# A transformer layer with linear attention: V products ahead of K in the head, fewer and longer dummy products, paced weight loads, and a newly searched order

## The chip, the cores and the metric

The kernel runs on one core of a Trainium2 chip. The metric is the device time of one execution in microseconds (us); it is measured several times and the median is taken. The core's engines are TensorE (PE, matrix products; its weight loads are listed as PEld), VectorE (DVE), ScalarE (ACT), GpSimd (POOL) and SyncE (SP, which here only issues transfers). Each engine works off its own list of instructions in order; between engines, semaphores make one wait for another.

## The reference

One layer over x of 2048 positions by 448 features, in bf16, with 16 heads of 28:

```python
qkv = (layernorm(x) @ wqkv)              # split into q, k, v per head
pq = einsum("bhsd,hdf->bhsf", q, w_phi)  # and pk from k, with the same w_phi
phi_q = concat([softmax(pq), softmax(-pq)], -1)   # phi_k likewise
kv = einsum("bhsf,bhsd->bhfd", phi_k, v)
z = einsum("bhsf->bhf", phi_k)
num = einsum("bhqf,bhfd->bhqd", phi_q, kv)
den = einsum("bhqf,bhf->bhq", phi_q, z)[..., None] + 1e-6
h = x + (num / den) @ wo
n = layernorm(h)
out = h + (sigmoid(n @ w_gate) * (n @ w_up)) @ w_down   # 448 -> 1792 -> 448
```

## The kernel before

The 2048 positions are 16 tiles of 128; four tiles make a chunk of 512. The names of the steps end in the number of their tile, or of chunk and part. The stages, as PE sees them:

- **Head.** The weights of K are transposed on PE (wT0 to wT3, copied out by wTe0 to wTe3), w_phi is spread on PE into a block matrix (wsp, masked by wex on DVE), and the product of the two, the folded weight, is made by w2m0_0 to w2m0_3 and cast to bf16 by w2e0_0 to w2e0_3. So K and w_phi are one product. The same is done for Q (w2m1_*, w2e1_*), whose weights come transposed by four transfers (ld_q0 to ld_q3, tile WqT). Meanwhile x is loaded (x0, x1, x2 ...), its statistics are taken (bst, agg on DVE), the reciprocal deviation made (pow1 on POOL) and the negated mean (nm1), x is normalized (xn) and transposed: tiles 0 to 3 on PE (xT0 to xT3, copied out by xT0e to xT3e), the others by transfers (xT4 to xT15 on SP's queue).
- **Keys and values, tiles 0 to 15.** For tiles 0 to 3 a pair of tiles shares a step: ppa0 and ppb0 are K of tiles 0 and 1, vva0 and vvb0 are V of tiles 0 and 1, ppa2 to vvb2 those of tiles 2 and 3. From tile 4 on, pva and pvb make K and V of one tile together. The a step has 8 products of 64 rows, run in pairs, and the b step 6. ACT takes both exponentials of K (ek), DVE sums and inverts them (ss, rs), POOL or DVE multiplies (phi), a copy brings V to SBUF (v1), and PE adds phi times V into two banks that stay open over all tiles (kva, kvb). At the end these are masked into kvz (kvzA to kvzD). One buffer of memory banks is shared by steps: ppa2 reuses the banks that ek0 and ek1 read, pva4 those that ek2 and v1_2 read.
- **Queries.** pqa and pqb make a chunk's part, ACT its two exponentials (eq, p and m for the signs). num makes numerator and denominator of a tile (rsm, qq, b, c, rden, o on DVE or POOL), o is transposed (oT, by PE for tiles 0 and 1, by transfers from tile 2), woa and wob multiply by wo; h, its statistics and norm follow (sq, ve, pow2, nm, hn), and its transpose hT (PE for tiles 0 and 1, transfers from tile 2).
- **Gate and up, down.** ga and gb make gate and up of a block of 128 features, ACT the tanh (sig), DVE the product (hh); dn, dp and dm multiply by w_down, fin adds the residual and out stores it.

What each engine does is written out by hand in `ORDER`, one list of names for each engine (lines 223 to 288). A step may run on one of several engines; it runs where its name stands. The dependences are worked out from the tiles that each step reads and writes, and waits are set for them; `PACE` adds dependences that no data asks for, here so that a weight load isn't issued too early. Steps whose function returns nothing (wwo, wgu) only make PE wait for weight loads. Dummy products of zeros (warm0 to warm9, line 524) fill PE in the head; each is n products of a given width:

```python
for i, (n, size) in enumerate(((4, 512), (1, 512), (1, 128), (2, 128), (1, 128), (6, 128), (4, 128), (6, 128), (8, 128), (2, 128))):
    op("pe", "warm%d" % i, warm(n, size), r=["zero"], w=[B(3)])
```

All products of two operands of 64 rows are issued by one helper, `both`, so that their line in the profile is L309.

Of the kernel before, what the change touches and what calls it, by code (L numbers as in the profile page):

```python
# [18 lines left out]
class Graph:  # L19
# [90 lines left out]
    def emit(self, nc):  # L110
# [111 lines left out]

ORDER = {
# [6 lines left out]
    ),  # L230
    "act": (
# [9 lines left out]
    ),  # L241
# [22 lines left out]
    ),  # L264
    "dve": (
# [14 lines left out]
    ),  # L280
    "pool": (
# [5 lines left out]
    ),  # L287
}
PACE = {"ld_wg1": "kva14"}
PROGRAM = (  # L290
# [35 lines left out]
def build(nc, A_x, A_wqkv, A_w_phi, A_wo, B_w_gate, B_w_up, B_w_down, out):  # L326
# [10 lines left out]
    with ExitStack() as es:  # L337
        def sb(name, shape, d=dt.bfloat16):
            return es.enter_context(nc.sbuf_tensor(name, shape, d))
        f32 = dt.float32  # L340
        ident = sb("ident", [P, P])
        zero = sb("zero", [P, 512])
        neghalf = sb("neghalf", [P, 4], f32)
        mask2 = sb("mask2", [P, 2], f32)
        par = sb("par", [P, 2])
# [10 lines left out]
        nm2 = sb("nm2", [P, NT], f32)  # L356
        ssq2 = sb("ssq2", [P, NT], f32)
        ve2 = sb("ve2", [P, NT], f32)
# [12 lines left out]
        zsel = sb("zsel", [GP, 452])  # L371
        hmask = sb("hmask", [GP, 4], f32)
# [148 lines left out]
        def warm(n, size):  # L521
            def f(e):
                for _ in range(n):
                    p = e.matmul(bk(3)[:, 0:size], lhsT=zero[:, 0:P], rhs=zero[:, 0:size], start=True, stop=True)  # L524
                return p
            return f
        for i, (n, size) in enumerate(((4, 512), (1, 512), (1, 128), (2, 128), (1, 128), (6, 128), (4, 128), (6, 128), (8, 128), (2, 128))):
            op("pe", "warm%d" % i, warm(n, size), r=["zero"], w=[B(3)])

        def evac(name, dst, src, rkey, wkey):  # L530
# [465 lines left out]
        at = {o.name: o.i for o in g.ops}  # L996
        for a, b in PACE.items():
            g.ops[at[a]].deps[at[b]] = False
# [36 lines left out]
```

## Time and profile before

| | us |
|---|---|
| median of 3 runs (lowest, highest) | 202.59 (202.31, 202.63) |
| the profiled execution | 202.7 |
| span of its instructions | 200.8 |
| PE busy | 195.5 |
| DVE busy | 132.0 |
| ACT busy | 89.4 |
| POOL busy | 56.2 |

The profile is of one execution; its span runs from the first instruction to the last, and the time of the execution holds some 2 us beside it. Line numbers (L309) are those of the kernel. A row of the timeline gives start, length, engine, line, operation, output and inputs, shapes, how many instructions are merged, and in brackets how long the engine was idle before and what released it. Products are pipelined, so a row's length is longer than what it adds before the next can start.

### The profile page before, as it was taken

What the parts mean: (1) busy time and instruction counts of PE and PEld (TensorE: products, weight loads), DVE (VectorE), ACT (ScalarE), POOL (GpSimd) and SP (SyncE); (2) the same over time, 40 slices, a digit from 0 to 9 for tenths busy, and PEclk for the clock granted to TensorE, in tenths of its full rate; (3) what the DMA queues carried; (4) which work ended last, traced back from release to release, by engine and by line L of the source; (5) the groups of instructions that cost most, each with busy time, mean ns of one, the idle gap of its engine ahead of it and who ended that gap; (6) DMA issues with size and microseconds to landing.
All of it is one profiled execution on the core that took longest, in us unless ns stands there. A gap on an engine that the chain in (4) does not pass through costs nothing.

```text
span 200.8 us, 5854 instructions
## 1 busy us (share of the span) xinstructions
PE 195.5 (97%) x2516; PEld 114.4 (57%) x2516; DVE 132.0 (66%) x308; ACT 89.4 (45%) x174; POOL 56.2 (28%) x95
## 2 busy tenths in 40 slices
PE   7999999999999999999999999999999999999995
PEld 4835556565568778787444444555555555554443
DVE  5999999978888986576569877346332422272224
ACT  2668988898883451434232432324323212222220
POOL 5779948633343207510170110001400000000000
PEclk9999999999999999999999999999999999999999
DMA  6965346749984230360015220020312000004002
GB/s 157 316 140 129 54 83 76 221 144 302 309 206 66 52 57 15 66 82 3 0 29 124 56 42 10 20 58 26 65 38 52 0 3 2 0 3 137 0 3 91
DMA packets 32490, 16.26 MB, mean 81 GB/s; under 512 B 24720, under 2 KB 31568, under 8 KB 32464
## 3 DMA queue, kind: packets, MB, share of 16 engines
q1 hardware_dynamic: 32336, 15.86, 33.7%
q8 instruction: 20, 0.33, 0.7%
q14 instruction: 6, 0.05, 0.1%
q10 hardware_dynamic: 128, 0.03, 0.1%
HBM read 8.34 MB, written 1.84 MB: 51 GB/s over the span
## 4 chain that ended last, share of the span: by engine, by line
PE 92%; ACT 3%; DMA 2%; issue 1%; SPq 1%; DVE 0%
PE psum L309 84%; PE psum L954 5%; DMA wk_sb<-in_A_wqkv_dram 2%; ACT hhT L671 1%; ACT eq L721 1%; ACT hhT L672 1%; PE psum L524 1%; PE psum L538 1%; PE psum L612 1%; SPq L413 1%; PE psum L599 0%; ACT xnT L531 0%; ACT v L531 0%; DVE x_sb L961 0%
## 5 line engine op out<-in xcount | busy, mean ns | idle before, releaser
L309 PE MATMUL psum<-xnT,wu_sb 64*128 64x512 bf16 (+1 forms) x490 | 93.6, 333 | 0.0
L309 PE MATMUL psum<-xnT,wg_sb 64*128 64x512 bf16 (+1 forms) x490 | 93.5, 333 | 0.1
L925 ACT ACTIVATE sg_sb<-psum 128x512 bf16<-128x512 f32 x56 | 33.2, 596 | 90.1 <-PE psum L309 89.5
L926 DVE SCALAR_TENSOR_TENSOR hhT<-sg_sb,psum 128x512 bf16<-128x512 bf16 x56 | 37.7, 684 | 52.1 <-ACT sg_sb L925 51.7
L309 PEld LDWEIGHTS psum<-xnT,wg_sb 64*128 64x128 bf16 x490 | 44.6, 94 | 20.9 <-DVE hhT L926 2.5
L309 PEld LDWEIGHTS psum<-xnT,wu_sb 64*128 64x128 bf16 x490 | 44.7, 94 | 13.9
L309 PE MATMUL psum<-wd_sb,hhT 64*128 64x448 bf16 x336 | 37.3, 349 | 0.0
L309 PEld LDWEIGHTS psum<-wd_sb,hhT 64*128 64x128 bf16 x336 | 17.8, 94 | 14.2 <-DVE x_sb L836 0.5
L309 PE MATMUL psum<-Wk,xnT 64*128 64x448 bf16 x112 | 22.2, 350 | 0.5 <-ACT hhT L672 0.2
L309 PE MATMUL psum<-wv_sb,xnT 64*128 64x448 bf16 x112 | 22.3, 351 | 0.1
L810 POOL TENSOR_TENSOR o_pad<-c_sb,rden 128x448 bf16<-128x448 bf16 x11 | 10.2, 935 | 28.5 <-DVE rden L806 28.4
L675 DVE TENSOR_REDUCE ss<-hhT 128x32 f32<-128x896 bf16 x16 | 16.8, 1060 | 0.2 <-ACT hhT L672 0.2
L721 ACT ACTIVATE eq<-psum 120x1024 bf16<-120x1024 f32 x16 | 15.6, 1030 | 0.6 <-PE psum L309 0.4
L685 POOL TENSOR_TENSOR phi<-hhT,rs 128x896 bf16<-128x896 bf16 x8 | 13.6, 1710 | 5.6 <-DVE rs L681 3.4
L309 PE MATMUL psum<-xnT,Wq 64*120 64x512 bf16 x112 | 14.8, 383 | 0.3 <-ACT eq L721 0.2
L845 POOL TENSOR_SCALAR ve<-ssq 128x1 f32<-128x1 f32 x11 | 2.2, 201 | 41.8 <-ACT junk L842 41.5
L309 PE MATMUL psum<-wo_o,oT 64*128 64x448 bf16 x56 | 13.2, 350 | 0.0
L309 PE MATMUL psum<-wo_e,oT 64*128 64x448 bf16 x56 | 13.2, 349 | 0.0
L961 DVE SCALAR_TENSOR_TENSOR x_sb<-psum,x_sb 128x448 bf16<-128x448 f32 (+2 forms) x17 | 9.4, 592 | 2.9 <-PE psum L954 1.6
L954 PE MATMUL psum<-wd_sb,hhT 128*128 128x448 bf16 (+2 forms) x70 | 11.2, 316 | 0.0
L309 PEld LDWEIGHTS psum<-Wk,xnT 64*128 64x128 bf16 x112 | 7.8, 94 | 5.8 <-PE psum L309 1.0
L671 ACT ACTIVATE hhT<-psum 128x448 bf16<-128x448 f32 x16 | 8.8, 553 | 4.4 <-PE psum L309 4.2
(105 smaller groups left out, 234.4 us busy)
## 6 DMA issues: line engine op xcount, KB each, us to landing
out_dram<-x_sb SPq DMA_DIRECT2D x15, 112.0 KB, 1.8
x_sb<-in_A_x_dram SPq DMA_DIRECT2D x7, 224.0 KB, 4.2
wd_sb<-in_B_w_down_dram SPq DMA_DIRECT2D x7, 224.0 KB, 5.1
wg_sb<-in_B_w_gate_dram SPq DMA_DIRECT2D x3, 448.0 KB, 5.8
wu_sb<-in_B_w_up_dram SPq DMA_DIRECT2D x3, 448.0 KB, 5.7
wv_sb<-in_A_wqkv_dram SPq DMA_DIRECT2D x2, 224.0 KB, 4.7
wk_sb<-in_A_wqkv_dram SPq DMA_DIRECT2D x2, 196.0 KB, 4.1
wo_e<-in_A_wo_dram SPq DMA_DIRECT2D x1, 336.0 KB, 3.3
```

The lines of the kernel that those rows point to most:

```text
L309: p = e.matmul(o, lhsT=w, rhs=r, start=st, stop=sp, tile_position=(row, 0))
L413: return op(eng, name, lambda e: e.dma_start(dst, src), r=r, w=w, dma="in" if eng == "sp" else "ain", nring=48 if eng == "sp" else 8, kb=kb)
L671: e.activation(ek[:, s, :, 0, :], src, ACT.Exp)
L675: op("dve", "ss%d" % t, lambda e: e.tensor_reduce(ss[:, s, :].rearrange("p (b h) -> p b h", h=2), eks.rearrange("p b (d h) -> p b h d", h= ...
L685: return e.tensor_tensor(phi[:, sp, :, :, :].rearrange("p b a n -> p (b a) n")[:, :, 0:56].rearrange("p b (d h) -> p b d h", h=2), eks.rea ...
L721: op("act", "eq%d_%d%s" % (c, i, "pm"[sg]), lambda e, sg=sg: e.activation(eq[c][:, sg, 2 * i:2 * i + 2, :].rearrange("p g n -> p (g n)"), ...
L810: return e.tensor_tensor(o_pad[:, t % NO, off:off + D].rearrange("p (h d) -> p h d", h=H), c_sb[:, t % NS, :, 0:DH], rden[:, t % NS, :][:, ...
L845: op(("pool", "dve"), "ve%d" % t, lambda e: e.tensor_scalar(ve2[:, t:t + 1], ssq2[:, t:t + 1], 1.0 / D ** 3, EPS, op0=ALU.mult, op1=ALU.ad ...
L925: op("act", "sig" + nm, lambda e: e.activation(sg_sb[:, k, 0:W], bk(bg)[:, 0:W], ACT.Tanh, scale=0.5), r=[B(bg)], w=[("sg", k)])
L926: op("dve", "hh" + nm, lambda e: e.scalar_tensor_tensor(out=dst, in0=sg_sb[:, k, 0:W].rearrange("p (f n) -> p f n", n=N), scalar=1.0, in1= ...
L954: p = e.matmul(bk(b)[:, lo:hi], lhsT=hb[:, ff, TS(t)], rhs=wd_sb[:, ff, lo:hi], start=ff == 0, stop=ff == FT - 1)
L961: op("dve", "fin%d%s" % (t, nm), lambda e: e.scalar_tensor_tensor(out=h_sb[:, t, lo:hi], in0=bk(b)[:, lo:hi], scalar=0.5, in1=h_sb[:, t, l ...
```

## The change

The products and transfers of data are the same ones; what differs is their order, the engine of some steps, the dummies and the holds.

- On SP's queue the two loads of V's weights (ld_v0, ld_v2) pass the loads x4 and x6.
- On PE, vva0 and vvb0 come ahead of ppa0 and ppb0, and vva2 ahead of ppa2 and ppb2 (vvb2 behind them); the transposes xT2 and xT3 and the folds w2m1_0 to w2m1_3 stand between other steps than before, all four folds ahead of pva4.
- The dummies are 14 products instead of 35, in 8 steps instead of 10; from the sixth step on they are 384 or 512 columns wide instead of 128. warm2 and warm3 stand ahead of wsp.
- `PACE` holds ten weight loads back instead of one, each until a named product (three of the loads of w_down follow the last two holds in SP's queue).
- Steps change engine: w2e0_3, v1_13, oT1e, nm1_1, nm1_4 and kvzC go to ACT; wTe3, phi8, o1, o10, o11, kvzB, ve5, ve8, ve9, hn4, hn6 and nm5 to DVE; phi5, phi6, o7, nm3, hn3, nm1_8, ve4 and ve6 to POOL.
- The order of many steps is new up to about num14 of PE's list; from there on PE's list is the same.

Cut to the head of each list, the queue of SP, PE's list up to num3 and around wgu, the holds and the dummies:

```diff
     "sp": (
-        "x0 x1 ld_k0 ld_k2 x2 x4 x6 ld_v0 ld_v2 x8 x10 ld_q1 ld_q0 ld_q3 ld_q2 x12 xT4 x14 xT5 xT6 xT7 xT8 xT9 xT10 "
+        "x0 x1 ld_k0 ld_k2 x2 ld_v0 ld_v2 x4 x6 x8 x10 ld_q1 ld_q0 ld_q3 ld_q2 x12 xT4 x14 xT5 xT6 xT7 xT8 xT9 xT10 "
...
     "act": (
-        "wphi wTe0 wTe2 wTe3 w2e0_0 w2e0_1 w2e0_2 par ek0 xT3e ek1 v1_0 v1_1 nm1_6 ek2 ek3 v1_2 w2e1_1 v1_3 nm1_8 "
-        "w2e1_0 v1_4 ek4 w2e1_2 ek5 v1_5 w2e1_3 v1_6 ek6 nm1_12 v1_7 ek7 ek8 v1_8 eq0_0p ek9 v1_9 ek10 v1_10 ek11 "
...
+        "wphi nm1_1 wTe2 wTe0 w2e0_1 w2e0_3 w2e0_2 w2e0_0 v1_1 v1_0 nm1_4 xT3e par ek0 ek1 nm1_6 w2e1_0 w2e1_1 ek2 "
+        "v1_2 ek3 v1_3 w2e1_3 ek4 v1_4 ek5 v1_5 w2e1_2 v1_6 ek6 nm1_12 ek7 v1_7 ek8 v1_8 eq0_0p ek9 v1_9 ek10 v1_10 "
...
     "pe": (
-        "warm0 warm1 wsp warm2 xT0 wT0 wT1 wT2 warm3 wT3 xT1 w2m0_0 w2m0_1 warm4 warm5 w2m0_3 w2m0_2 warm6 warm7 "
-        "warm8 ppa0 ppb0 warm9 xT2 xT3 vva0 vvb0 ppa2 ppb2 vva2 seed vvb2 w2m1_0 w2m1_1 kva0 pva4 kvb0 pvb4 pva5 "
-        "w2m1_2 w2m1_3 pvb5 kva1 pva6 kvb1 kva2 pvb6 kvb2 pva7 pqa0_0 pvb7 pva8 kva3 pvb8 kvb3 pqb0_0 pva9 kva4 pvb9 "
...
-        "kvb14 kva15 kvb15 qs pqa1_1 num0 num1 pqb1_1 pqa2_0 num2 pqb2_0 pqa2_1 oT0 oT1 num3 pqb2_1 woa0 wob0 pqa3_0 "
-        "num4 pqb3_0 pqa3_1 pqb3_1 num5 hT1 hT0 woa2 ga0_2 ga0_0 ga0_1 num6 gb0_0 ga0_3 gb0_1 gb0_2 gb0_3 wob2 num7 "
...
-        "wob6 gb0_10 ga0_12 gb0_11 ga0_13 dn0_0 dn0_4 gb0_12 gb0_13 num9 ga2_2 ga2_3 dn0_8 gb2_2 gb2_3 ga2_0 ga2_1 "
...
+        "warm0 warm1 warm2 warm3 wsp xT0 wT1 warm4 wT2 wT3 wT0 warm5 xT1 w2m0_1 w2m0_3 warm6 warm7 w2m0_2 w2m0_0 vva0 "
+        "vvb0 ppa0 xT3 ppb0 xT2 vva2 w2m1_0 ppa2 w2m1_1 ppb2 vvb2 seed w2m1_3 w2m1_2 kva0 pva4 pvb4 pva5 kvb0 kva1 "
+        "pvb5 pva6 kvb1 kva2 pvb6 pva7 pqa0_0 pvb7 pva8 kvb2 kva3 pvb8 kvb3 pqb0_0 pva9 kva4 pvb9 pva10 kvb4 kva5 "
...
+        "pqa1_1 num0 pqb1_1 num1 pqa2_0 num2 pqb2_0 pqa2_1 oT1 oT0 pqb2_1 num3 woa0 wob0 pqa3_0 num4 pqb3_0 pqa3_1 "
+        "wgu pqb3_1 num5 hT1 hT0 woa2 ga0_2 ga0_0 ga0_1 num6 ga0_3 wwo gb0_0 gb0_1 gb0_2 gb0_3 wob2 num7 ga0_4 ga0_5 "
...
+        "wob6 ga0_12 ga0_13 num9 gb0_12 gb0_13 dn0_0 dn0_4 dn0_8 ga2_2 num10 ga2_3 dn0_11 ga2_0 ga2_1 dp0_0 gb2_0 "
...
     "dve": (
-        "zero hmask mask2 bst0 agg0 bst1 agg1 xn0 kvzones wex xT0e wTe1 bst2 bst3 xT1e agg3 w2e0_3 agg2 bst7 bst5 "
-        "bst4 xn2 agg5 agg4 agg7 bst6 xT2e agg6 ss0 bst8 rs0 bst9 bst10 bst11 ss1 agg8 agg9 rs1 agg11 agg10 ss2 phi1 "
...
-        "rsm7 rden6 qq7 h2 b7 h3 c7 rden7 o7 hh0_4 ve3 hh0_6 h4 nm2 h5 nm3 rsm8 hn2 hn3 qq8 hh0_8 h6 h7 b8 c8 rden8 "
...
+        "zero hmask mask2 bst0 agg0 bst1 agg1 xn0 wex wTe1 xT0e wTe3 bst2 bst3 xT1e agg2 agg3 bst5 bst4 bst6 agg5 "
+        "agg6 agg4 bst7 xn2 agg7 bst10 agg10 xT2e bst8 ss0 bst9 rs0 ss1 agg9 agg8 bst11 rs1 agg11 ss2 phi1 rs2 bst14 "
...
+        "h2 b7 h3 c7 nm2 rden7 hh0_4 hh0_6 h4 ve3 rsm8 h5 qq8 b8 c8 hn2 hh0_8 h7 h6 rsm9 qq9 rden8 hh0_10 nm4 b9 c9 "
...
     "pool": (
-        "ident0 steps phipad ident zsel neghalf pow1_0 opad0 pow1_1 nm1_1 xn1 epsl0 v1ones wqpad epsr0 pow1_3 nm1_3 "
-        "pow1_2 xn3 pow1_4 nm1_4 xn4 pow1_6 xn5 xn6 phi0 xn7 pow1_8 xn8 phi2 xn10 xn9 phi4 pow1_12 xn13 phi7 xn15 "
...
+        "ident0 steps phipad ident zsel neghalf opad0 wqpad epsr0 epsl0 pow1_0 v1ones pow1_1 xn1 nm1_3 pow1_3 xn3 "
+        "pow1_2 pow1_4 xn4 pow1_6 xn5 xn6 phi0 xn7 nm1_8 pow1_8 xn8 phi2 xn9 xn10 phi4 pow1_12 phi5 xn13 phi6 phi7 "
+        "xn15 phi9 phi10 phi13 o0 o2 o3 pow2_0 pow2_1 o4 o5 o6 nm3 o7 ve2 pow2_3 hn3 pow2_2 ve6 ve4 pow2_4 o9 ve7 "
...
-PACE = {"ld_wg1": "kva14"}
+PACE = {"ld_wg0": "pvb14", "ld_wu0": "pvb15", "ld_wg1": "kvb10", "ld_wu1": "kvb11", "ld_wg2": "kvb12", "ld_wu2": "kvb13", "ld_wg3": "kvb14",
+        "ld_wu3": "pqa1_1", "ld_wd0": "num1", "ld_wd2": "pqb1_1"}
...
-        for i, (n, size) in enumerate(((4, 512), (1, 512), (1, 128), (2, 128), (1, 128), (6, 128), (4, 128), (6, 128), (8, 128), (2, 128))):
+        for i, (n, size) in enumerate(((4, 512), (1, 512), (1, 128), (2, 128), (1, 128), (2, 384), (1, 512), (2, 384))):
```

71 rows, old and new, of the table ORDER are left out of this document.

## The prediction

> **What bounds the kernel now.** I read the page first, then stretches of the span, then the chain that ended last, then the timeline of the first 20 us engine by engine.
>
> ```profile
> span 200.8 us, 5854 instructions
> PE 195.5 (97%) x2516; PEld 114.4 (57%) x2516; DVE 132.0 (66%) x308; ACT 89.4 (45%) x174; POOL 56.2 (28%) x95
> 8.00:18.00 10.00, 9.46 (x114) 5.03 (x112) 9.80 (x27) 7.26 (x19) 8.32 (x12) 1.00 0.80 187
> 18.00:43.00 25.00, 24.98 (x426) 14.98 (x428) 24.63 (x48) 22.26 (x50) 17.72 (x15) 1.00 0.53 120
> 43.00:60.00 17.00, 16.28 (x303) 9.96 (x301) 13.98 (x39) 14.54 (x20) 5.74 (x7) 1.00 0.91 241
> 60.00:125.00 65.00, 64.90 (x950) 42.08 (x946) 48.98 (x130) 23.08 (x48) 16.25 (x29) 1.00 0.27 48
> 125.00:201.00 76.00, 73.41 (x676) 37.85 (x670) 29.15 (x54) 19.31 (x36) 3.04 (x8) 1.00 0.12 33
> ```
>
> The stretches give, after their length, busy time of PE, weight loads, DVE, ACT, POOL, then granted clock and DMA. PE is idle 0.02 us between 18 and 43 and 0.10 us between 60 and 125, at a granted clock of 1.00, so there the time is PE's list of products and no order of it helps. What can be gained lies before 18 us, where PE is kept busy partly by dummies (products of zeros, L524), and between 43 and 60 us, where PE is idle 0.72 us. DVE is as full as PE from 8 to 43 us (9.80 of 10 and 24.63 of 25): a lead won in the head survives only if DVE can be earlier too.
>
> ```profile
> 8.59 1.01 PE psum L524 x18
> 9.59 0.92 PE psum L309 x8
> ...
> 17.45 0.43 ACT v L531
> 17.89 0.14 issue
> 18.02 2.49 PE psum L309 x30
> ...
> 47.20 1.95 ACT eq L721 x2
> ...
> 49.19 1.07 PE psum L309 x8
> ...
> 58.21 65.46 PE psum L309 x960
> ```
>
> The chain (start, length, what) shows three places. At 8.59 it runs through a whole microsecond of dummies, until the keys of tiles 0 and 1 (ppa0) may start. At 18.02 pva4 starts, released by ACT's copy of V of tile 2 (v1_2). At 49.19 PE was waiting for the exponentials of the queries (eq, ACT).
>
> **The head, walked again.** The rows for it:
>
> ```profile
> 1.17 2.31 PE L524 MATMUL psum<-zero 128*128 128x512 bf16 x5 [1.17 <-DVE zero L417]
> 6.39 0.41 PE L599 MATMUL psum<-ident,wk_sb 112*112 112x112 bf16 x4 [0.16 <-DMA wk_sb<-in_A_wqkv_dram]
> 6.70 1.15 DVE L545 BATCH_NORM_STATS2 st<-x_sb 128x6 f32<-128x448 bf16 x2
> 7.19 0.61 PE L612 MATMUL psum<-Wphi,WkT 112*128 112x112 bf16 x8
> 7.69 1.72 ACT L531 CAST Wk<-psum 128x448 bf16<-128x448 f32 x3
> 7.77 0.41 DVE L531 COPY xnT<-psum 128x512 bf16<-128x512 bf16 x1
> 9.56 1.74 PE L309 MATMUL psum<-Wk,xnT 64*128 64x448 bf16 x14
> 11.34 0.54 ACT L671 ACTIVATE hhT<-psum 128x448 bf16<-128x448 f32 x1 [1.88 <-PE psum L309]
> 11.78 0.54 ACT L672 ACTIVATE hhT<-psum 128x448 bf16<-128x448 f32 x1
> 13.82 1.74 PE L309 MATMUL psum<-Wk,xnT 64*128 64x448 bf16 x14 [0.19 <-ACT hhT L672]
> 15.64 1.69 POOL L685 TENSOR_TENSOR phi<-hhT,rs 128x896 bf16<-128x896 bf16 x1
> 17.05 0.57 PE L612 MATMUL psum<-Wphi,WqT 112*128 112x112 bf16 x8
> 17.31 0.57 ACT L531 CAST v<-psum 128x448 bf16<-128x448 f32 x1
> ```
>
> *Dummies ahead of the spread of w_phi.* The first five dummies of 512 columns took 2.31 us with a drain of 0.2, some 0.42 each, so three of 128 moved ahead of it (warm2, warm3) cost 3 x 0.105 = 0.32 us at most. They end nothing: the transposes wT2 and wT3 wait at 6.39 for the second load of the keys' weights, and nothing that the spread delays is needed for them. If that load were 0.3 us earlier, this cover would be gone and 0.3 us the price. The 384-wide dummies, not in the trace, lie between 0.06 us (18 of 128 in 1.01) and 0.42 us; I take 0.16, three quarters of a 512 at the later, doubled rate.
>
> *Start of V.* From 6.39: three transposes of weights (0.2 each to issue), two 384-dummies (0.33), xT1 (0.22), four folds (the row at 7.19 has two, eight products, in 0.61 with the drain, so 0.2 each) and the three dummies warm6 and warm7 (0.53): 6.39 + 0.6 + 0.33 + 0.22 + 0.8 + 0.53 = 8.9. The other input of vva0 is xT1's copy: DVE now has wTe3 first (to 7.4), two statistics (1.15 less an overlap of 0.1), then that copy (0.41): 8.84. So V of tiles 0 and 1 starts at 8.9, where dummies stood, instead of K at 9.56.
>
> *Keys behind it.* A 14-product pair step issues in 1.6 us: 8.9 + 1.6 = 10.5 for ppa0. It needs all four casts of the folded weight, now all on ACT: three in a row took 1.72, so about 0.52 each: from the first fold's end at 7.97, done at 10.2, hidden under V by 0.3 us. K ends near 12.25 (the 1.74 of the row at 9.56), so the first exponential starts at 12.4 instead of 11.34, a loss of 1.06. Two tiles of exponentials (11.34 and 11.78 rows: 0.98 for one, overlapping a little) end at 14.25, and ppa2, which reuses their banks, starts at 14.3 instead of 13.82. PE is idle about 0.65 us before vva2 (xT2's copy) and 0.4 us before ppa2, which the before filled with work.
>
> *The gain of the order.* K of tile 2 ends at 16.0. ACT then does ek2, v1_2, ek3 instead of ek2, ek3, v1_2: 16.05 + 0.87 + 0.57 = 17.45 for v1_2, against 17.88. With the 0.14 us from copy to product that the chain shows, pva4 starts at 17.6 instead of 18.02: 0.42 earlier. By then all four folds of the queries' weights are done, where the before had done two; the other two stood behind pva5, 0.2 us each (17.05 row: two folds in 0.57 with the drain). The lead of PE's list at pva4 is 0.42 + 0.4 = 0.8 us. kva0 stands ahead of pva4 and needs phi0 (POOL, 1.69 long). Even started as late as before, at 15.64, it ends at 17.33, so it does not hold pva4.
>
> **What else moves in the head.**
>
> ```profile
> 4.05 0.94 SPq L413 DMA_DIRECT2D wv_sb<-in_A_wqkv_dram  x2
> 6.03 5.16 SPq L503 DMA_TRANSPOSE WqT<-in_A_wqkv_dram  x4
> wv_sb<-in_A_wqkv_dram SPq DMA_DIRECT2D x2, 224.0 KB, 4.7
> DMA to landing us min/median/max: 3.7/4.4/5.0
> ```
>
> On SP's queue V's two loads pass x4 and x6: issued 0.95 us earlier, the second near 3.6, and landing by 3.6 + 4.7 = 8.3, ahead of 8.9; without the move the second would land near 9.2 and V would wait 0.3 us. x4 and x6 take V's old place and with the same 4.7 land near 8.8 and 9.2; their statistics come at 9.0 and 10.0, behind xT1's copy and tile 3's mean: nothing, and 0.5 us if DVE were there earlier. The transposes of the queries' weights (last row: their time to landing) keep their place; the last issue is near 9.9, so they land by 13.6 to 14.9. The fold w2m1_0 now stands ahead of ppa2, at 13.7: between nothing and 0.8 us of wait; I take 0.1, since ppa2 itself may not start before 14.3.
>
> **From 18 to 60 us.**
>
> ```profile
> 36.53 0.62 DVE L531 CAST v<-psum 128x448 bf16<-128x448 f32 x1
> 42.22 1.14 DVE L685 TENSOR_TENSOR phi<-hhT,rs 128x896 bf16<-128x896 bf16 x2
> 45.86 0.63 PE L309 MATMUL psum<-kvz,eq 56*128 56x60 bf16 x32
> 50.63 0.58 ACT L531 COPY oT<-psum 128x512 bf16<-128x512 bf16 x1 [0.58 <-PE psum L538]
> 46.33 0.44 SPq L413 DMA_DIRECT2D wu_sb<-in_B_w_up_dram  x1
> wu_sb<-in_B_w_up_dram SPq DMA_DIRECT2D x3, 448.0 KB, 5.7
> 70.24 3.37 SPq L856 DMA_TRANSPOSE xnT<-hn_pad  x2
> 75.67 0.27 PE L309 MATMUL psum<-xnT,wg_sb 64*128 64x256 bf16 x1
> ```
>
> *DVE* starts its statistics of tiles 2 and 3 some 0.66 us later (7.36 for 6.70), but gives a cast of the folded weight (about 0.57, as ACT's) and one of V (0.53) to ACT, and phi5 and phi6 to POOL for phi8 (net 0.55). It ends phi15 about 1 us earlier, at 42.4, and PE wants it about 2 us ahead of num0 (45.86 before): at 42.9 with the lead. POOL pays 1.7 us for the added phi out of 7.3 idle (17.72 of 25); ACT pays a V copy of 0.55 out of 2.7 idle. So the 0.8 us carries through. kvb0 and kva1, and kvb2 and kva3, now stand together; no row prices that, between nothing and 0.2 us, and I take 0.1.
>
> *At 46 us* pqb1_1 passes num1 (two num steps issue in 0.45, so 0.22 each): the exponentials that the chain waits for start 0.2 us earlier. oT1's copy moves to ACT (0.58), whose idle time of 0.58 before that copy and 2.5 in the stretch (14.54 of 17) hides it; o1 goes from POOL to DVE. If ACT had no idle left there, the 0.58 would be the price.
>
> *The ten paced loads.* SP now waits for pvb14 to pqb1_1; behind it stand only the rest of the weights and the transposes of o, far later. The last gate or up load is issued after pqa1_1, which ends just ahead of num0: 44.9 now against 46.33, landing 5.7 later, near 50.6. PE asks for all of them (wgu) ahead of pqb3_1, some 1.7 us of steps before the row of 58.21, so near 55.4 with the lead. Cost nothing, 4.8 us of cover; gain nothing either.
>
> **The sum.** 0.8 + 0.1 + 0.2 = 1.1 us off a span of 200.8: 199.7. The profiled execution took 202.7, 1.9 more than its span, and the median is 202.59: I predict 201.5. From num14 on, PE's order is the same, so nothing is given back by the tail as written.
>
> **The rivals.**
>
> *The lead stops at DVE, ACT or the queries' transposes (chance 0.14).* DVE had 0.37 us of room in 25. If its list or ACT's exponentials run 0.5 to 1 us later than I walked, or w2m1_0 waits the 0.8 us, what remains is 0 to 0.4: 202.2 to 202.6, no change that can be measured (0.2%, 0.4 us, is about what a measurement of this kernel tells). For it: the first exponential is 1.06 us later. Against it: V's copies, formerly behind it, are already done.
>
> *Slower: hT3 late (0.10).* nm3 and hn3 move to POOL, behind o7, and hn2 behind c8, while ga2_2, which reads both transposes, keeps its place by the queue of PE and is reached 0.9 us earlier, near 74.8. The before issued hT2 and hT3 from 70.24 to 73.61 and used them at 75.67, so hT3 landed with 0 to 2.06 us to spare. It decides when hT3 lands after 74.8; each 0.1 us from there is 0.1 us of PE. If there was no margin and POOL's longer steps add 1 us, PE stands 75.67 + 1 - 74.8 = 1.9 us: 203.4. Against it: what hn2 and hn3 read is itself computed earlier with the lead.
>
> *Slower: the clock (0.06).* 0.42 us for 512 columns early, then 0.056 for 128, is a doubled rate. With 14 dummies for 35 and PE idle for 1.05 us in the 2 us around 13, the rate could halve: the 2.6 us of products up to 16.4 would take 2.6 more, 0.4 hidden behind ACT: 203.7. Against it: in the before the rate held between 6.4 and 7.2, which is nearly all transposes behind a wait, and through the wait of 0.19 at 13.82. [...]
>
> **How the numbers follow.** Forecast 0.70: 201.5, and between 200.8 (all of the 0.72 idle in 43 to 60 goes, and of that 0.2 is counted already, plus the 0.2 taken as 0.1 and nothing for w2m1_0) and 202.1 (the 0.5 us of the added dummies' and casts' bounds lost). No change 0.14, slower 0.16. The range from 200.8 to 202.8 takes in the rival of no change, with the 0.2 by which runs of before spread, and leaves out the slower ones and a little below.
>
> **What would show it.** Right: the first V product near 8.9, ppa0 near 10.5, the first exponential near 12.4, pva4 near 17.6, num0 near 44.9, the chain's wait for eq at 48.0, PE still full from 60 on. Wrong: pva4 not before 18.0; idle PE of over 0.2 us between 18 and 43; ga2_2 waiting for the transpose of hn; products of 512 columns at 0.42 us after 10 us.

## The result and the profile after

The changed kernel took 206.17 us (median; 205.21 to 206.59, 4 executions) against 202.45 us of the kernel before beside it. The ratio is 1.0178, interval 1.0162 to 1.0195: slower by 3.7 us, where 1.1 us of gain were forecast. Two executions at a mean granted clock of 0.992 took 206.6 and 206.5 us, two at 1.000 took 205.2 and 205.8. The profiled one is the first, with a span of 204.8. In what follows, an execution more than 1.5% above the fastest of its kernel is left out of the ratio, but not out of the median and the range: one of the kernel before with ten holds (206.32) and two of the same with 20 dummies fewer (206.79 and 205.86).

The page of the profile after, cut to its size, the granted clock in 40 slices of 5.1 us, and the packets of PE's own list of instructions (queue 8: how many, MB, share of the transfer engines):

```profile
span 204.8 us, 5810 instructions
...
PEclk9999999999699999999999999999999999999999
...
q8 instruction: 19, 0.31, 0.7%
```

The same stretches as before (length; busy PE, weight loads, DVE, ACT, POOL; granted clock, DMA):

```profile
8.00:18.00 10.00, 8.66 (x97) 4.11 (x94) 9.13 (x27) 7.72 (x21) 8.29 (x12) 1.00 1.08 195
18.00:43.00 25.00, 24.37 (x418) 14.04 (x416) 24.79 (x45) 22.09 (x49) 19.51 (x16) 1.00 0.51 118
43.00:60.00 17.00, 14.56 (x246) 8.86 (x246) 11.12 (x30) 12.03 (x18) 3.36 (x4) 0.90 0.65 186
60.00:125.00 65.00, 64.84 (x972) 41.34 (x970) 50.85 (x137) 25.53 (x50) 15.73 (x28) 1.00 0.30 62
125.00:201.00 76.00, 75.90 (x693) 38.77 (x690) 30.35 (x58) 20.51 (x38) 3.03 (x8) 1.00 0.10 27
```

PE is idle 0.63 us between 18 and 43 (before 0.02) and 2.44 us between 43 and 60 (before 0.72). The granted clock is 0.90 in that last stretch, and PE got through 246 products there instead of 303. From 60 us on it is full, as before. The chain that ended last (start, length, what) names three places:

```profile
10.01 4.21 DMA WqT<-in_A_wqkv_dram
...
29.19 1.38 DVE kvz L462
...
31.72 0.97 DVE xn_pad L574
...
35.63 0.05 issue
...
44.84 1.58 PE psum L310 x48
46.42 0.11 issue
46.54 2.90 PE psum L310 x65
49.44 1.92 issue
51.35 2.28 PE psum L310 x11
```

The queries' transposed weights hold the head (10.01). Two small DVE steps take some 1.9 us together more than usual (29.19, 31.72; their rows stand below). And at 49.44 PE stands for 1.92 us, with nothing in the profile that it waited for. That stop is in the middle of a step, as PE's timeline shows:

```profile
48.80 0.64 PE L310 MATMUL psum<-xnT,Wq 64*120 64x512 bf16 x3
51.35 2.28 PE L310 MATMUL psum<-xnT,Wq 64*120 64x512 bf16 x11 [1.92 <-issue]
53.56 1.03 PE L539 MATMUL psum<-ident,o_pad 128*128 128x128 bf16 x8
54.53 1.20 PE L310 MATMUL psum<-xnT,Wq 64*120 64x512 bf16 x6
55.80 0.35 PE L310 MATMUL psum<-x_sb,ident 64*128 64x448 bf16 x2
```

The rows hold pqb2_0 (6 products) and pqa2_1 (8). pqb2_0 has issued 3 of its 6 products and had every input that it needs, yet the other 3, and the 8 of pqa2_1 behind them, come 1.9 us later. Products and transposes are slow behind that: the granted clock is 0.50 from 51.84 to 55.25 us. woa0, the row at 55.80, stood at 51.66 before: 4.14 us late. num0 (46.54) had been 0.68 us late. From woa0 to the end of the span both kernels need 149.0 to 149.1 us.

### The profile page after: what moved, and what is told of

It reads as the page before. It is cut to its first block, busy times and chain, and to the rows that moved or that the text cites. A ratio compares the mean times of both kernels' runs of the same rounds, so it can differ in the third digit from the quotient of the medians.

```text
span 204.8 us, 5810 instructions
## 1 busy us (share of the span) xinstructions
PE 196.4 (96%) x2494; PEld 112.8 (55%) x2495; DVE 133.2 (65%) x309; ACT 91.1 (44%) x177; POOL 54.5 (27%) x91
## 4 chain that ended last, share of the span: by engine, by line
PE 81%; DVE 9%; SPq 4%; DMA 2%; issue 2%; ACT 0%
PE psum L310 75%; PE psum L955 5%; DVE ss L676 4%; SPq L414 2%; DMA WqT<-in_A_wqkv_dram 2%; SPq L504 2%; DVE phi L686 1%; DVE st L546 1%; DVE rs L682 1%; DVE xn_pad L574 1%; PE psum L539 1%; DVE kvz L462 1%; PE psum L613 0%; ACT hhT L672 0%; ACT hhT L673 0%
## 5 line engine op out<-in xcount | busy, mean ns | idle before, releaser
L811 POOL TENSOR_TENSOR o_pad<-c_sb,rden 128x448 bf16<-128x448 bf16 x9 | 8.4, 938 | 37.9 <-DVE rden L807 21.0
L310 PE MATMUL psum<-xnT,Wq 64*120 64x512 bf16 x112 | 16.2, 406 | 2.1 <-issue 1.9
L676 DVE TENSOR_REDUCE ss<-hhT 128x32 f32<-128x896 bf16 x16 | 16.6, 1049 | 0.3 <-ACT hhT L673 0.3
L686 POOL TENSOR_TENSOR phi<-hhT,rs 128x896 bf16<-128x896 bf16 x9 | 15.3, 1707 | 5.1 <-DVE rs L682 2.7
L802 DVE TENSOR_TENSOR b_sb<-psum,qq 128x464 bf16<-128x464 f32 x16 | 10.2, 636 | 0.7 <-PE psum L310 0.5
```

Of the source, the lines that this page charges most:

```text
L310: p = e.matmul(o, lhsT=w, rhs=r, start=st, stop=sp, tile_position=(row, 0))
L676: op("dve", "ss%d" % t, lambda e: e.tensor_reduce(ss[:, s, :].rearrange("p (b h) -> p b h", h=2), eks.rearrange("p b (d h) -> p b h d", h= ...
L686: return e.tensor_tensor(phi[:, sp, :, :, :].rearrange("p b a n -> p (b a) n")[:, :, 0:56].rearrange("p b (d h) -> p b d h", h=2), eks.rea ...
L802: op("dve", "b%d" % t, lambda e: e.tensor_tensor(h3(b_sb), OMv[:, :, :, 0:EV], h2(qq)[:, :, :, None].to_broadcast([P, NB, 8, EV]), ALU.mul ...
L811: return e.tensor_tensor(o_pad[:, t % NO, off:off + D].rearrange("p (h d) -> p h d", h=H), c_sb[:, t % NS, :, 0:DH], rden[:, t % NS, :][:, ...
```

## What stopped PE: the theory and its rivals

The stop falls where PE's list of instructions, by the packets of its queue, should have been refilled. That queue delivers 0.31 MB in 19 packets, 16 KB each, for 4,989 products and weight loads: one packet for about 260 of them. That queue 8 carries PE's list is read from this: its packets keep pace with PE, and all kernels of the study with 42 or 44 more of PE's instructions have 20 of them, the others 19. In the records of single packets, those around the stop come at 30.20, 37.65, 43.18, 50.76 us before and at 30.04, 40.26, 48.85, 52.62 after. Between 40.26 and 48.85 PE worked off some 400 instructions without a refill, and it stopped at the end of these. The transfers of that time in the changed kernel (41.4 to 48.8 us):

```profile
DMA packets 659, 2.05 MB, mean 278 GB/s; under 512 B 86, under 2 KB 86, under 8 KB 659
...
q1 hardware_dynamic: 659, 2.05, 100.7%
```

No packet of instructions is among them; the transfer engines are full with weights. Before, the same place (42.6 to 44.2 us) is empty but for the refill:

```profile
DMA packets 4, 0.02 MB, mean 15 GB/s; under 512 B 1, under 2 KB 1, under 8 KB 3
...
q8 instruction: 1, 0.02, 3.6%
q1 hardware_dynamic: 3, 0.01, 1.1%
```

*Theory:* the refill stands behind the ten paced loads, which leave no pause, and PE runs dry. The old single hold at kva14 had left a pause (SP began one load at 37.70 us and the next at 43.57), and the refill, due at about PE's 1,220th instruction, fell into it. That place is an estimate: the packet of before and those of two of the kernels below start within 0.4 us of PE's 1,222nd instruction, semaphores counted. Fewer dummies (21 products less and their weight loads, 42 instructions) make it due later, deeper among the loads: 44.05 us for 42.93, and 43.30 in the kernel below that gets as many instructions back. *Rivals:* the loads are innocent and PE is late by DVE; or the order of the steps decides and not the place in the list.

## The experiments

**The old hold.** The changed kernel with `PACE` of before:

```diff
-PACE = {"ld_wg0": "pvb14", "ld_wu0": "pvb15", "ld_wg1": "kvb10", ... "ld_wd2": "pqb1_1"}
+PACE = {"ld_wg1": "kva14"}
```

> The changed kernel with the one hold of before (the second gate load until kva14) in place of the ten. Theory refill: PE's idle 1.92 us at 49.4 is a late refill of its own instruction list (16 KB packets on a queue of kind instruction: 48.85 where before had one at 43.18), held up by weight loads that now run from 38 to 55 us without a pause; with the old hold the idle time and the half rate behind it (both together 3.4 us by the starts of woa0) go, and what is left is the 0.7 us that PE was late at num0: 203.2 us, between 202.8 and 203.6. Rival order: the new lists themselves make PE stand there, the holds being harmless: 206 as the changed kernel.

Measured 203.34 us (203.15 to 203.43), ratio 1.004 (1.0026 to 1.0053): 2.8 us of the loss are gone. The stretch:

```profile
43.00:60.00 17.00, 16.31 (x298) 9.86 (x294) 14.53 (x40) 15.52 (x22) 4.86 (x6) 1.00 0.85 228
```

The stop is gone and the clock is 1.00. A refill came at 46.13 us, 2.0 us after it was due. From num0 to woa0 it took 5.77 us instead of 9.26. The other 0.9 us are still lost.

**The kernel before with the ten holds.** The same edit the other way round, on the kernel before:

> The kernel before, with the ten holds of the change and nothing else of it. Theory refill: the loads run without a pause from 38 us, the refill asked for near 43 us comes late by several us, and PE runs dry near 50: an idle time of 1 to 2.5 us with no releaser and then products at half rate, 204.5 to 206.5 us. Rival order: within 0.4 us of before, 202.0 to 202.9.

Measured 202.83 us (202.14 to 206.32, 10 executions), ratio 1.0015 (0.9993 to 1.0037). Most of the expectation missed: the same ten holds cost the old list little. In the profiled execution the refill was due at 42.51 and came at 44.29, in time. The loads alone don't do it, at least not in most executions; the one of 206.32 had a mean clock of 0.992, like two of the changed kernel, and has no profile.

**The kernel before without any hold.** `PACE = {}`:

> The kernel before without its one hold, so that the eight gate and up loads and three of w_down follow each other from 37 us. Theory refill: the packet of before at 43.18 must queue behind them, PE runs dry between 44 and 50 us: idle time without a releaser of 1 us or more, 204 to 206.5 us. Rival order: the hold of before did nothing, 202.0 to 202.9.

Measured 205.13 us (203.08 to 206.05), ratio 1.0114 (1.0051 to 1.0178). PE's waits:

```profile
PE psum L309 <- issue: 2.3, 1, 2.3
```

The stop appears in the old list as well. Loads were issued without a pause from 36.7 us on, and the refill came at 47.06.

**The square of holds and dummies.** With ten holds, old order and old dummies run at 202.8 and new order and new dummies at 206.2. Two kernels fill the other corners. The first is the changed kernel with 22 dummies of 32 columns in a place where PE waits anyway:

```diff
-... (2, 384), (1, 512), (2, 384))):
+... (2, 384), (1, 512), (2, 384), (22, 32))):
-"... w2m0_2 w2m0_0 vva0 "
+"... w2m0_2 w2m0_0 warm8 vva0 "
```

> The changed kernel, ten holds and all, with 22 dummies of 32 columns ahead of vva0: 44 more instructions in PE's list, as many as before the change. Theory (the refill of PE's list is due at a place in the list; the nearer that is to the first of the paced loads, the fewer loads stand in its way): it is due about 1 us earlier than in the changed kernel, as in the kernel before with ten holds, which mostly ran at 202.8; most runs near 203.3 (the changed kernel with the single hold), some near 206, median under 204.5. Rival (the ten holds in this order alone decide, and 44 instructions do not matter): 206.2 as the changed kernel.

Measured 203.59 us (203.35 to 204.56), ratio 1.0054 (1.0032 to 1.0076). Products of zeros and nothing else take off 2.6 us, and the trace has no stop. The transfers between 44.0 and 46.5 us:

```profile
q1 hardware_dynamic: 217, 0.70, 99.8%
q8 instruction: 1, 0.02, 2.7%
```

The weight loads are as dense as in the changed kernel, and the refill, due at 43.30 instead of 44.05, gets through at 45.93 instead of 48.85. The second corner is the kernel before with ten holds and 20 dummies fewer:

```diff
-... (1, 128), (2, 128), (1, 128), (6, 128), (4, 128), (6, 128), (8, 128), (2, 128))):
+... (1, 128), (1, 256), (1, 128), (2, 384), (1, 512), (2, 384), (2, 512))):
```

> The kernel before with the ten holds and 20 dummies fewer (the same columns in fewer and longer dummies, but for 256 columns): 40 instructions fewer in PE's list, the order of before otherwise. Theory: the refill falls due about 0.9 us later, among more loads, and PE runs dry near 48 us: median 204.5 to 206. Rival (the order, not the place in the list): 202.8, as with the ten holds alone.

Measured 204.28 us (206.79, 203.86, 205.86, 204.28, 202.81). The ratio is 1.0048 (1.0015 to 1.008). PE's waits and its chain in the profiled one, 206.79:

```profile
PE psum L310 <- issue: 3.1, 1, 3.1
```

```profile
46.00 2.04 PE psum L310 x32
48.03 3.12 issue
51.15 1.92 PE psum L310 x13
```

The stop is there with the old order of steps, as in the kernel before without any hold. How many products and weight loads (x, under PE and under its weight loads) PE had started when it stood, in the three traces with a stop, the changed kernel, the one without any hold and this one:

```profile
0.00:49.20 49.20, 45.42 (x723) 26.54 (x725) 44.02 (x95) 38.49 (x81) 32.45 (x52) 1.00 0.72 167
0.00:47.06 47.06, 44.90 (x723) 27.07 (x723) 42.25 (x94) 36.37 (x78) 31.23 (x51) 1.00 0.76 170
0.00:48.47 48.47, 45.65 (x723) 27.00 (x723) 43.84 (x98) 37.62 (x79) 31.67 (x52) 1.00 0.72 168
```

PE stands each time at the same place of its list, after 1,446 to 1,448 of them, and each time in the middle of a step: ahead of the 4th product of pqb2_0, the 6th of pqa2_0 and the 2nd of pqb2_0. It goes on 2.50, 2.60 and 2.68 us after the start of the late packet (48.85, 47.06, 48.47). So it takes both: loads without a pause and a refill that falls due late among them. That decides for the place in the list and against the order of the steps. How much the 20 dummies cost in the old order stays open: the ratio overlaps the 1.0015 (0.9993 to 1.0037) of the same kernel with all its dummies.

**Where the lead went: DVE and POOL.** With the old hold in place, kvzones goes back to the head of DVE's list:

> As the changed kernel with the old hold, and kvzones (24 elements a row, DVE) back behind xn0. Theory port: kvzones took 1.45 us between ss7 and rs7 where it took 0.21 in the head, because a long step of POOL (phi6, over at 30.48) ran and kvzones ended right behind it at 30.56; early it costs 0.2 and DVE is 1.2 us less late at phi8, so that PE's wait of 0.40 us for phi8 at 35.3 and of 0.22 at 44.5 go: 0.5 to 0.7 us below the changed kernel with the old hold, 202.4 to 202.8. Rival: DVE meets the long steps of POOL with the next short step instead (rs7, xn14) and gains under 0.2 us: 203.1.

Measured 203.17 us (202.02 to 204.52), ratio 1.0034 (1.0011 to 1.0057), too spread to tell 0.2 us. The trace tells why little was won: the step behind kvzones met the next of POOL's long products. First the rows of the changed kernel, DVE, then POOL:

```profile
27.77 0.42 DVE L574 TENSOR_SCALAR xn_pad<-x_sb,mv,rst 128x512 bf16<-128x512 bf16 x1
...
29.11 1.45 DVE L462 CAST kvz<-mask 128x24 bf16<-128x24 f32 x1
...
31.64 1.05 DVE L574 TENSOR_SCALAR xn_pad<-x_sb,mv,rst 128x512 bf16<-128x512 bf16 x1
```

```profile
28.80 1.68 POOL L686 TENSOR_TENSOR phi<-hhT,rs 128x896 bf16<-128x896 bf16 x1
30.85 1.69 POOL L686 TENSOR_TENSOR phi<-hhT,rs 128x896 bf16<-128x896 bf16 x1 [0.37 <-DVE rs L682]
```

A cast of 24 columns (kvzones) takes 1.45 us and ends at 30.56, POOL's phi6 at 30.48. xn14 takes 1.05 us, for 0.32 to 0.50 of the other four of its kind, and ends at 32.69, phi7 at 32.54. So each of the two ends within 0.15 us behind the end of the product beside it; what ties them is not shown. Not every step of DVE is longer there: the sums ss (L676) beside the same products take their usual 1.02 to 1.08 us. In the kernel with kvzones early, xn14 ran from 29.78 to 31.63 against a phi7 that ended at 31.48. So the next edit gives the products back to the engines of before (phi5 and phi6 to DVE, phi8 to POOL; a few short steps of DVE change places with that). The author forecast 201.4 for it, if DVE's steps beside POOL's products come back near their usual length:

```diff
-dve:  ... ss6 rs6 xn12 ss7 rs7 ss8 xn14 rs8 ss9 ss10 rs9 phi8 rs10 ss11 ...
+dve:  ... ss6 xn12 rs6 ss7 phi5 phi6 xn14 rs7 ss8 ss9 rs8 ss10 rs9 rs10 ss11 ...
-pool: ... pow1_12 phi5 xn13 phi6 phi7 xn15 phi9 ...
+pool: ... pow1_12 xn13 phi7 xn15 phi8 phi9 ...
```

> The order after the change with the single hold of before, kvzones in the head, and the assignment of the phi products of before (phi5 and phi6 on DVE, phi8 on POOL). [...] Rival (POOL's extra product costs DVE nothing, DVE is simply later by its own work): two phis of 0.57 more and one less on DVE make phi15 0.5 us later, num0 near 46 and 202.6. Theory of the refill: with the single hold at kva14 the refill of PE's list is due within 0.5 us of the release of the loads, so the runs are spread over 1 us or more.

Measured 202.78 us (202.02 to 203.35), ratio 1.0006 (0.9987 to 1.0026): no difference from the kernel before that can be told. The stretch:

```profile
18.00:43.00 25.00, 24.77 (x426) 14.46 (x420) 24.65 (x47) 22.66 (x49) 18.60 (x16) 1.00 0.51 122
```

PE is idle 0.23 us there instead of 0.63, and num0 comes 27.46 us after pva4 instead of 28.39. The cast takes 0.20 us in the head and xn14 takes 0.79 us, instead of 1.45 and 1.05, and phi15 starts at 42.85 us instead of 43.72, although DVE has one product more to make. So in the trace both steps are shorter, as forecast. The time of 201.4 was not reached; the median is nearer to the rival's 202.6.

**The wait in the head.** In the kernel with the phis back, the folds of the queries' weights move behind ppa2, the last two behind kva1 (their casts in ACT's list move with them):

```diff
-... vva2 w2m1_0 ppa2 w2m1_1 ppb2 vvb2 seed w2m1_3 w2m1_2 kva0 pva4 pvb4 pva5 kvb0 kva1 pvb5
+... vva2 ppa2 w2m1_0 ppb2 vvb2 seed w2m1_1 kva0 pva4 pvb4 pva5 kvb0 kva1 w2m1_3 w2m1_2 pvb5
```

> As the kernel with the phis back, and the folds of the queries' weights behind ppa2, the last two behind kva1. Theory (PE waits 0.3 to 0.5 us for the transposed load of WqT in the head, and that wait is on the path): 0.3 us faster than the same kernel with the folds ahead of ppa2, num0 near 44.5, about 201.1. Rival (ppa2 may not start before ACT has released its banks in any case): the same time within 0.2 us.

Measured 202.74 us (202.23 to 204.24), ratio 1.0023 (1.0004 to 1.0043): the same as with the phis back, as the rival said. What took the place of the wait for WqT:

```profile
14.77 0.93 PE L309 MATMUL psum<-Wk,xnT 64*128 64x448 bf16 x8 [0.17 <-ACT hhT L672]
```

ppa2 now waits for ACT to release its banks.

**A later hold, and 44 instructions more, on the best order.** The kernel with the folds behind ppa2 and `PACE = {"ld_wg1": "kvb15"}`, wgu behind ga4_2:

> As the kernel with the folds behind ppa2, but the loads of gate and up are held until kvb15 instead of kva14, and PE asks for them later (wgu behind ga4_2, as before the change). Theory (the refill of PE's list, due near instruction 1222, must pass ahead of the queued loads): the refill is now always issued before the loads are released, so the runs spread by less than 0.6 us around 201.2, none above 202.2, and the trace shows no idle PE without a releaser. Rival (the spread comes from elsewhere): the spread of 1 us or more stays. Rival (the loads are now late): PE waits for wg at ga0_2, about 0.5 us or more.

Measured 203.16 us (202.74 to 204.82), ratio 1.0044 (1.0019 to 1.0069). The spread did not narrow, and something else is late, which neither theory had named:

```profile
59.44 0.35 PE L309 MATMUL psum<-wo_e,oT 64*128 64x448 bf16 x1 [0.91 <-DMA oT<-o_pad]
```

The transposes oT2 and oT3 are issued no later than with the hold at kva14 (53.42 us for 53.54), but the slowest of o's transposes now takes 5.4 us to land for 4.2, while the loads, released 0.7 us later (44.81 for 44.10), still run; that these slow it is argued and not tested. And the kernel with the phis back and the 22 dummies of 32 columns:

> As the kernel with the phis back (hold at kva14, folds ahead of ppa2), with 22 dummies of 32 columns ahead of vva0, which add 44 instructions to PE's list as before the change and little time of PE there (it waits for xT1's copy). Theory (the refill is due at a place in the list, so 44 more instructions let it fall due about 1 us earlier, ahead of the release at kva14): the spread of the runs falls below 0.7 us, at the best time of the kernel with the phis back or up to 0.3 more for the dummies. Rival (the refill is due by time, or the spread is not from it): the same spread as the kernel with the phis back.

Measured 202.78 us (202.16 to 203.12), ratio 1.0009 (0.9996 to 1.0022): same median, a spread of 1.0 us for 1.3, not the 0.7 expected. Its profiled execution shows another late transpose:

```profile
76.46 0.27 PE L309 MATMUL psum<-xnT,wg_sb 64*128 64x256 bf16 x1 [0.47 <-DMA xnT<-hn_pad]
```

So the spread of these orders is not mainly from the refill. Its source stays open; a late transpose is seen twice, in one execution each.

**The forecast gain at 46 us.** The kernel before with pqb1_1 ahead of num1:

> The kernel before with one step moved: pqb1_1 ahead of num1, as the change has it. If the 0.2 us that the prediction gave to this is right: 202.25, within 0.2 either way; if the wait for the exponentials is set by ACT's list and not by pqb1_1, 202.45 as before.

Measured 202.41 us (202.03 to 204.07, 12 executions), ratio 0.9998 (0.9979 to 1.0017). The forecast 0.2 us can't be told from nothing. No kernel of the study is faster than the one before by more than the noise.

## Why the prediction was wrong, point by point

- **"The ten paced loads. Cost nothing, 4.8 us of cover": this is the step that failed.** Its size was 2.8 us (changed kernel less the one with the old hold). The cover was counted for PE's use of the weights, and there it held: nothing waits for wg. What waited was not a step at all: the refill of PE's list on the same transfer engines, which the page of before shows as one line (`q8 instruction: 20, 0.33, 0.7%`). It came 4.8 us after it was due, and PE stood for 1.92 us and then ran at half the clock for 3.41 us. The wait that the change took away (SP standing at kva14) was not costed as the pause that it was.
- **"Dummies fewer and longer" were priced by their columns.** Their number counted too: 22 dummies put back, in a place where they cost PE nothing, are worth 2.6 us. That is nearly the same 2.8 us again, not a further loss, since either edit avoids the stop.
- **"DVE ends phi15 about 1 us earlier", "POOL pays 1.7 us for the added phi out of 7.3 idle": wrong sign.** This is a second step that failed: it was to carry the lead through. phi15 started at 43.72 (42.74 before), 1 us later and not earlier. Idle time of POOL wasn't free for DVE: beside its products of 1.68 and 1.69 us the cast took 1.45 us (0.20 in the head) and xn14 1.05 us (0.79 with the phis back). PE waited 0.40 us for phi8 at 35.68 and 0.22 us for phi15 at 44.49, and lost 0.93 us between pva4 and num0 against the order with the phis back; the medians give 0.56 us (203.34 less 202.78) for the two edits together, kvzones early and the phis back.
- **The head: the walk was close, the lead wasn't.** V started at 8.60 (forecast 8.9), ppa0 at 10.17 (10.5), the first exponential at 12.13 (12.4), the wait for xT2's copy took 0.72 (0.65). But w2m1_0 waited until 14.36, where 0.1 us had been taken from a range of 0 to 0.8, and 0.28 was the wait. ppa2 came 0.35 late, pva4 at 18.15 instead of 17.6. With two folds more done (0.4 us), that is a lead of 0.3 us for the forecast 0.8, in a head whose start moves by some 0.5 us either way between executions: V started between 8.35 and 9.32 in the kernels with this order. (The 17.45 for v1_2 adds up to 17.49; nothing hangs on it.)
- **The rivals.** "The lead stops at DVE, ACT or the queries' transposes" (0.14) comes nearest to what the kernel with the phis back shows, 202.78, a little above its 202.2 to 202.6. "The clock" (0.06) had the right kind of event at the wrong place: not at 13 us, where the granted clock stayed at 1.00 with the 14 dummies, but behind the stop at 49, where it was 0.50 for 3.41 us. Here pqb2_0 to woa0 lost 1.92 us by standing and some 1.6 us by slow products. "hT3 late" (0.10) didn't happen in the changed kernel; the kernel of the 22 dummies with the phis back shows it, at 0.47 us.
- **At 46 us**, the 0.2 us for pqb1_1 ahead of num1 can't be told from nothing (202.41 for 202.44 beside it).
- **The tail.** "Nothing is given back" held: 149.0 us from woa0 to the end against 149.1.

The 3.7 us add up as 2.8 for the stop with its slow clock, 0.6 for DVE's longer steps beside POOL (medians, the second of kernels that spread by 1.3), and 0.3 for what is left of the order against the one before, which is within what these runs can tell.

## What to carry to other kernels

PE's list of instructions came here over the transfer engines too, in 19 or 20 packets of 16 KB, and with the weight loads at 100.7% of these engines one packet came 4.8 us after it was due and PE stood for 1.92 us. So when a change closes a pause among large loads, or shifts the count of instructions ahead of it, look where such packets fall and how far the list gets without them (some 250 instructions here). A hold that seems to cost transfer time can be what lets something small pass: with the one at kva14 SP began no load between 37.70 and 43.57 us, and the packet of 43.18 us passed. And when work is moved to GpSimd, its idle time is not the whole price (phi6, 1.68 us long, had a VectorE cast beside it that took 1.45 us for 0.20): look at which small VectorE steps will stand beside its long ones.

## What the runs showed of the hardware that wasn't expected

- A refill of PE's list that is due among dense weight loads came 1.8 us (old order, ten holds), 2.6 us (22 dummies added), 4.6 us (before without a hold), 4.8 us (changed kernel) and 5.3 us (20 dummies fewer) after it was due, each counted from PE's 1,222nd instruction. In the last three, where PE had worked off some 250 more instructions by then, it stopped for 2.30, 1.92 and 3.12 us. What sets the length of the refill's own wait was not tried.
- The stops of 1.92 and 3.12 us were each followed by 3.41 us at a granted clock of 0.50, the stop of 2.30 us was not. The groups of query products in the two stretches, the changed kernel (48.5 to 55.6 us):

```profile
L310 PE MATMUL psum<-xnT,Wq 64*120 64x512 bf16 x24 | 4.7, 489 | 1.9 <-issue 1.9
```

and the kernel before without a hold (46.0 to 53.4 us):

```profile
L309 PE MATMUL psum<-xnT,Wq 64*120 64x512 bf16 x34 | 4.7, 384 | 2.3 <-issue 2.3
```

The mean product is 489 ns in the one and 384 ns in the other. So the length of the stop alone doesn't decide it; what does stayed open. By an estimate from these figures, 3.41 us at half the clock make the mean of some 205 us 0.992. Eight executions have 0.991 or 0.992: two of four of the changed kernel, two of four without a hold, two of five with 20 dummies fewer, and one of ten each with ten holds and with the old hold and kvzones early; of the kernel before, none of the 68 beside the experiments has it. Only two of the eight are profiled, both with the stop, so that the others had it too is not shown.
- A VectorE cast of 24 columns, 0.2 us in the head, took 1.45 us beside GpSimd's product of 1.68 us.
